# A two-layer recurrent transformer on one core: whole-unit loops become a hand-written order of pieces, with half-size weight loads

## The chip, the cores and the metric

The kernel runs on one core of a Trainium2 chip. The time is device microseconds from the first to the last instruction, as the median of several executions. Times inside the kernel are from a hardware profile of one execution. Engine names are those of the profile: PE is TensorE (matmuls), PEld its weight loads, DVE the vector engine, ACT the scalar engine, POOL is GpSimd, and SP the queue that issues the weight transfers.

## What is computed

There are two kinds of layer, A and B, applied as A, B, A, B, each with a layer norm before it and a residual after it. The sequence is 2048 tokens of 640 numbers. A is a memory-augmented attention that runs over the sequence in 64 segments of 32 tokens; the first 8 output rows of a segment are the memory that goes in front of the next segment, so the segments follow one another:

```python
for s in range(n_seg):                                   # 64 segments
    h = concat([mem, x[:, 32*s : 32*s+32]])              # 8 + 32 rows of 640
    q, k, v = h @ Wq, h @ Wk, h @ Wv                     # 32 heads of 192
    p = softmax(where(mask, q @ k.T * 192**-0.5, -1e9))
    o = (p @ v) @ Wo                                     # back to 640
    mem, out = o[:, :8], o[:, 8:]
```

B is a sliding attention with 32 heads of 20: each token looks at itself and the 7 tokens 2, 4, ... 14 places before it. Both A layers use the same weights, and so do both B layers. Inputs and weights are bf16. A's four weight matrices hold 31.5 MB[...], so part of them is read again for every segment.

## The kernel before

**Lanes and steps.** The two A layers are run at once, as two lanes of one step: lane 0 works on segment t of the first A layer, lane 1 on segment t-2 of the second. One step t does A for both lanes (80 columns: 2 x 40 rows) and B for the step before (64 columns). Steps 0 and 1 have only lane 0, steps 64 and 65 only lane 1, and step 66 has only B. The 62 steps between are full.

**Units.** A's 32 heads are handled as 8 groups of 4 heads (`NQUAD`). For each group i there are four weight units of 960 KB: K, Q, V and O. A projection (`proj_stationary`) is 30 matmuls with a fresh 128x128 weight block each, into one PSUM bank. Of the 32 units, every other one in order of use is resident on chip after the first step (`resident_units`, 16 units); the other 16 come in each step through a ring of four buffers (`RING`). The SP queue issues these loads in order of use, each one as soon as its buffer's last reader is done (`unit`).

**One group of heads.** K is copied out of PSUM by ACT into `KF` and `Kz` (L223 to L225), Q by DVE (`QT`, L230), V by ACT (`VT`, L236). V is transposed by six TensorE instructions (`a_vt`, L242) and copied by DVE (`Vt`, L246). Scores are eight matmuls (`a_s`, L256 and L257), then an exponential on ACT (`E`, L259) and a mask on DVE (`Em`, L261). `a_pv` sums the denominators by a matmul with ones (L270), multiplies `Em` by `Vt` (L275), takes the reciprocal of the denominators as two ACT operations (`R`, L278 and L279) and scales into `OT` with three DVE operations (L281 to L283). `a_o` is 30 matmuls that add into one accumulator bank, `acc` (L294).

**The end of a step.** When the last `a_o` is done, `mem_out` copies the memory rows of `acc` into the next step's input `hT` (L309), and `b_x1` adds the residual (L355). The next step's first K projection needs these memory rows. The layer norm for the next step's tokens (`ln1_sq`, `ln1`, `ln1_r`, `ln1_apply`) lies in the last group.

**Order.** The instruction order is the program's order, engine by engine (`manual_schedule`). `step` writes it as a loop over the groups: K, Q, V of group i, the output matmuls of group i-2, the transposes of V of group i, PV of group i-1, the scores of group i, with B's parts put in at fixed groups. Each function issues its matmuls and at once the ACT and DVE work that takes them out of PSUM. The output matmuls of the last three groups come together at the end:

```python
self.a_vt(7)
self.a_o(5, (0, 2, 3, 5))
...
self.a_pv(7)
self.a_o(5, (1, 4))
self.a_o(6)
self.a_o(7)
```

Most PSUM results rotate over four banks (`big`); scores, denominators, PV and `acc` have a bank each.

Of the kernel before, what the change touches and what calls it, by code (L numbers as in the profile page):

```python
# [17 lines left out]
P = 128  # L18
# [20 lines left out]
N_UNITS = 32  # L39
N_RES = 16  # L40
RING = 4

def unit_order():
    order = []
    for i in range(NQUAD):
        order.append(("k", i))
        order.append(("q", i))
        order.append(("v", i))
        if 2 <= i < NQUAD - 1:
            order.append(("o", i - 2))  # L50
    order += [("o", 5), ("o", 6), ("o", 7)]
    return order

def resident_units():
    res = set()
    for n, u in enumerate(unit_order()):
        if (n * N_RES) // N_UNITS != ((n + 1) * N_RES) // N_UNITS:
            res.add(u)
    return res

class Kernel:
    def __init__(self, ctx, tc, xT, m0T, wA, wqkv, wo, out):
        self.tc = tc
        self.nc = tc.nc
        self.x = xT
        self.mem0 = m0T
        self.wA = wA
        self.b_src = (wqkv, wo)
        self.out = out
        self.n_seg = 4 * xT.shape[0]  # L70
        pool = lambda name, bufs, **kw: ctx.enter_context(tc.tile_pool(name=name, bufs=bufs, **kw))
        self.cp = pool("consts", 1)
        self.wres = pool("wres", 1)
        self.wring = pool("wring", RING)
        self.ap2 = pool("act2", 2)
        self.ap3 = pool("act3", 3)
        self.bp = pool("bact", 1)
        self.xp = pool("xio", 1)
        self.ps_big = pool("ps_big", 4, space=PSUM)
        self.ps_one = pool("ps_one", 1, space=PSUM)  # L80
        self.units = {}
        self.held = (None, None)
        self.place = {u: n for n, u in enumerate(unit_order())}
        self.resident = resident_units()
        self.build_consts()

    def build_consts(self):
# [31 lines left out]
        self.On = pers("On", [P, 3 * P], 1)[0]  # L119
        self.YT = pers("YT", [P, NC, P], 1, zero=False)[0]  # L120
# [55 lines left out]
    def unit(self, kind, i):  # L176
        if (kind, i) in self.units:
            return self.units[(kind, i)]
        if self.held[0] == (kind, i):
            return self.held[1]  # L180
        res = (kind, i) in self.resident
        if res:
            t_ = self.wres.tile([P, 3840], BF16, name=f"w_{kind}{i}")
        else:
            t_ = self.wring.tile([P, 3840], BF16, name="w_ring")
        self.nc.sync.dma_start(out=t_[:], in_=self.wA[self.place[(kind, i)]])
        v = t_[:].rearrange("p (a b) -> p a b", a=6 if kind == "o" else NC)
        if res:
            self.units[(kind, i)] = v
        self.held = ((kind, i), v)  # L190
        return v

    def big(self, name):
        return self.ps_big.tile([P, 512], F32, name=name, tag="big")
# [9 lines left out]
    def proj_stationary(self, kind, i, t):  # L204
        nc = self.nc
        w = self.unit(kind, i)
        hT = self.hT[t % 2]
        ps = self.big(f"ps_{kind}")
        c0, c1 = self.cs.start, self.cs.stop
        for n in range(6):  # L210
            for c in range(NC):
                nc.tensor.matmul(ps[:, NT * n + c0:NT * n + c1], lhsT=w[:, c, P * n:P * (n + 1)], rhs=hT[:, NT * c + c0:NT * c + c1],  # L212
                                 start=(c == 0), stop=(c == NC - 1))
        return ps

    def a_k(self, i, t):
        nc = self.nc
        ps = self.proj_stationary("k", i, t)
        pv = ps[:, 0:6 * NT].rearrange("p (a b n) -> p a b n", a=2, b=3)
# [7 lines left out]
    def a_q(self, i, t):  # L227
        ps = self.proj_stationary("q", i, t)
        qt = self.ap2.tile([P, 6, NT], BF16, name="QT")
        self.nc.vector.tensor_copy(out=qt[:, :, self.cs], in_=ps[:, 0:6 * NT].rearrange("p (a n) -> p a n", a=6)[:, :, self.cs])  # L230
        self.qt = qt

    def a_v(self, i, t):
        ps = self.proj_stationary("v", i, t)
        vt = self.VT[i % 2][:, 0:6 * NT].rearrange("p (a n) -> p a n", a=6)
        self.nc.scalar.copy(out=vt[:, :, self.cs], in_=ps[:, 0:6 * NT].rearrange("p (a n) -> p a n", a=6)[:, :, self.cs])  # L236

    def a_vt(self, i):
        nc = self.nc
        ps = self.ps_big.tile([P, 6, P], BF16, name="ps_vt", tag="big")  # L240
        for n in range(6):
            nc.tensor.transpose(out=ps[:, n, :], in_=self.VT[i % 2][:, NT * n:NT * n + P], identity=self.ident[:])  # L242
        src = ps[0:NT].rearrange("p n e -> p (n e)").rearrange("p (a j e) -> p a j e", a=2, j=2)
# [4 lines left out]
    def a_s(self, i):  # L248
# [3 lines left out]
        kf, kz, qt = self.KF[i % 2], self.Kz[i % 2], self.qt  # L252
        cs, w = self.cs, self.cs.stop - self.cs.start
# [4 lines left out]
        e = self.ap2.tile([P, 4, NT], BF16, name="E")  # L258
        nc.scalar.activation(out=e[0:NT, :, cs], in_=sv[0:NT, :, cs], func=ACT.Exp, scale=float(DH) ** -0.5)  # L259
        em = self.ap2.tile([P, 4, NT], BF16, name="Em")  # L260
        nc.vector.tensor_tensor(out=em[0:NT, :, cs], in0=e[0:NT, :, cs], in1=self.maskA[0:NT, cs].unsqueeze(1).to_broadcast([NT, 4, w]), op=ALU.mult)  # L261
        self.em = em

    def a_pv(self, i):
        nc = self.nc
        em = self.em
        vt = self.Vt[i % 2]
        cs = self.cs
        dn = self.one("d")[:, 0:4 * NT].rearrange("p (h n) -> p h n", h=4)[:, :, cs]
        nc.tensor.matmul(dn, lhsT=self.ones[0:NT, :], rhs=em[0:NT, :, cs], start=True, stop=True)  # L270
        ops = self.one("o")
        ov = ops[:, 0:6 * NT].rearrange("p (a b n) -> p a b n", a=2, b=3)
        for pr in range(2):
            for (b, w0, j, st, sp) in [(0, 0, 0, True, True), (1, 128, 0, True, False), (1, 256, 1, False, True), (2, 384, 1, True, True)]:
                nc.tensor.matmul(ov[:, pr, b, cs], lhsT=vt[0:NT, 512 * pr + w0:512 * pr + w0 + P], rhs=em[0:NT, 2 * pr + j, cs], start=st, stop=sp)  # L275
        r = self.ap2.tile([P, 2, 2, NT], F32, name="R")
        rf = r[:].rearrange("p a b n -> p (a b) n")[:, :, cs]
        nc.scalar.activation(out=rf, in_=dn, func=ACT.Ln)  # L278
        nc.scalar.activation(out=rf, in_=rf, func=ACT.Exp, scale=-1.0)  # L279
        ot = self.ap3.tile([P, 2, 3, NT], BF16, name="OT")  # L280
        nc.vector.tensor_tensor(out=ot[:, :, 0:3:2, cs], in0=ov[:, :, 0:3:2, cs], in1=r[:, :, :, cs], op=ALU.mult)  # L281
        nc.vector.tensor_tensor(out=ot[0:64, :, 1, cs], in0=ov[0:64, :, 1, cs], in1=r[0:64, :, 0, cs], op=ALU.mult)
        nc.vector.tensor_tensor(out=ot[64:P, :, 1, cs], in0=ov[64:P, :, 1, cs], in1=r[64:P, :, 1, cs], op=ALU.mult)  # L283
        self.ots[i] = ot

    def a_o(self, i, ms=(0, 2, 3, 5, 1, 4)):
        nc = self.nc
        w = self.unit("o", i)
        ot = self.ots[i][:].rearrange("p a b n -> p (a b) n")
        if i == 0:  # L290
            self.acc = self.one("acc")
        for m in ms:
            for c in range(NC):
                nc.tensor.matmul(self.acc[:, NT * c + self.cs.start:NT * c + self.cs.stop], lhsT=w[:, m, P * c:P * (c + 1)], rhs=ot[:, m, self.cs],  # L294
                                 start=(i == 0 and m == ms[0] and c == 0), stop=(i == NQUAD - 1 and m == ms[-1]), skip_group_check=True)
# [4 lines left out]
    def mem_out(self, t):  # L300
        nc = self.nc
        a = self.lanes(self.acc[:, 0:NC * NT])
        h = self.lanes(self.hT[(t + 1) % 2][:, 0:NC * NT])
        if t + 1 == LAG:
            nc.vector.tensor_copy(out=h[:, :, 0, 0:NM], in_=a[:, :, 0, 0:NM])
            nc.vector.tensor_copy(out=h[:, :, 1, 0:NM], in_=self.m0T[:])
# [43 lines left out]
    def b_x1(self, b):  # L350
# [6 lines left out]
        self.bsq = self.ln_sq(x1)  # L357

    def b_ln(self, b):
        self.bmr = self.ln_r(self.ln_mv(self.ln_stats(self.x1[b % 2], self.bsq)))  # L360
# [15 lines left out]
    def b_k(self, b):  # L376
        ps = self.b_proj(b, D, "ps_bk")
        self.nc.scalar.copy(out=self.KB[:, :, 64 * (b % 2):64 * (b % 2) + NX], in_=ps[:, 0:NBC * NX].rearrange("p (a n) -> p a n", a=NBC))

    def b_q(self, b):  # L380
        ps = self.b_proj(b, 0, "ps_bq")
        qb = self.bp.tile([P, NBC, NX], BF16, name="QB")
        self.nc.scalar.copy(out=qb[:], in_=ps[:, 0:NBC * NX].rearrange("p (a n) -> p a n", a=NBC))
        self.qb = qb

    def b_v(self, b):
# [8 lines left out]
        nc.scalar.copy(out=self.VTB[:, :, hs], in_=ps[:, 0:NC * NX].rearrange("p (a n) -> p a n", a=NC))  # L395

    def b_vt(self, b):
        nc = self.nc
        ps = self.ps_big.tile([P, NC, P], BF16, name="ps_bvt", tag="big")
        for n in range(NC):  # L400
            nc.tensor.transpose(out=ps[:, n, :], in_=self.VTB[:, n, :], identity=self.ident[:])
        hs = slice(64 * (b % 2), 64 * (b % 2) + NX)
        src = ps[hs].rearrange("p n e -> p (n e)").rearrange("p (a h d) -> p a h d", a=2, d=BD)
# [3 lines left out]
    def b_qexp(self, g):  # L407
        nc = self.nc
        qx = self.ap2.tile([P, 2, BHC, NX], BF16, name="QX")
# [5 lines left out]
        if g == 0:  # L415
            self.eb = self.bp.tile([P, BH // 2, 2, NX], BF16, name="EB")

    def b_s(self, b, c):
# [4 lines left out]
        e = self.ap2.tile([P, BHC, NX], BF16, name="eraw")  # L423
        nc.scalar.activation(out=e[:, 0:nh, :].rearrange("p h n -> p (h n)"), in_=ps[:, 0:nh * NX], func=ACT.Exp, scale=float(BD) ** -0.5)
# [9 lines left out]
    def b_pv(self):  # L434
        nc = self.nc
        W = 2 * BD + 1
        on = self.On[:, 0:D // 2].rearrange("p (h d) -> p h d", d=BD)
# [212 lines left out]
```

The softmax here doesn't subtract the row's maximum and nothing guards it: scores larger than these inputs give would overflow.

## Time and profile before

| | before |
|---|---|
| time, median of 4 runs | 3675.62 us (3668.48 to 3692.0) |
| span of the profiled execution | 3672.8 us |
| PE busy, weight loads busy | 3290.7 us (90%), 3160.4 us (86%) |
| DVE, ACT busy | 2039.3 us (56%), 1713.3 us (47%) |
| moved by DMA | 1074.62 MB, mean 293 GB/s |
| loads through the ring | 1056 of 960 KB, 5.9 us to landing at the median |
| mean granted TensorE clock | 0.986 |

Matmuls are pipelined: one is shown with about 200 ns, but the next starts some 36 ns later, so the busy share of PE hides short gaps. The chain of work that ended last counts each piece of TensorE work once, from start to the next start, and names what was waited for in the gaps; "issue" in it is time in which the engine waited for nothing that the profile shows. A line of the list of waits gives the engine and line that stood idle, what ended the wait, the total, the number of times and the longest.

### The profile page before, as it was taken

To read this page: it belongs to the slowest core of one execution; us is meant where nothing else is said; L and a number is where in the kernel's file an instruction comes from. 1 tells how busy PE (TensorE), PEld (TensorE's weight loads), DVE (VectorE), ACT (ScalarE), POOL (GpSimd) and SP (SyncE) were. 2 spreads that over 40 slices of the span, in tenths; PEclk is the share of its full clock that TensorE was granted. 3 is DMA by queue.
4 is the path that set the end of the run, shared out by engine and by line. 5 is a ranking of instruction groups with operands and counts; after the bars stand their busy time and mean duration, and the time that the engine had idled before them with its cause. 6 is when DMAs were issued, how large, how long until landed. Compare 5 with 4: busy or idle time off the path is not lost.

```text
span 3672.8 us, 188119 instructions
## 1 busy us (share of the span) xinstructions
PE 3290.7 (90%) x86394; PEld 3160.4 (86%) x86394; DVE 2039.3 (56%) x6223; ACT 1713.3 (47%) x4621; POOL 40.7 (1%) x150
## 2 busy tenths in 40 slices
PE   4899899999999999999999999998999998999987
PEld 4788888888988888988988888888888988888886
DVE  2455555555555555555555555555555555555554
ACT  1344444444444444544544444444444544444443
POOL 1000000000000000000000000000000000000000
PEclk7899999999999999999999999999999999999998
DMA  9887888878888888888888888888878888878785
GB/s 391 299 290 286 285 298 294 294 286 302 294 290 294 290 289 293 300 291 298 301 288 301 290 293 287 294 292 285 294 285 292 298 286 289 298 287 289 287 290 213
DMA packets 160201, 1074.62 MB, mean 293 GB/s; under 512 B 17840, under 2 KB 21936, under 8 KB 159280
## 3 DMA queue, kind: packets, MB, share of 16 engines
q1 hardware_dynamic: 154656, 1057.33, 79.9%
q8 instruction: 676, 11.08, 1.2%
q10 hardware_dynamic: 4752, 5.26, 0.4%
q14 instruction: 117, 0.96, 0.1%
HBM read 1059.89 MB, written 2.62 MB: 289 GB/s over the span
## 4 chain that ended last, share of the span: by engine, by line
PE 83%; DVE 6%; issue 5%; ACT 4%; DMA 2%; POOL 0%; POOLq 0%; SPq 0%; ACTq 0%; DVEq 0%
PE ps_k L212 15%; PE ps_v L212 15%; PE ps_acc L294 14%; PE ps_q L212 14%; PE ps_vt L242 5%; PE ps_o L275 4%; ACT VT L236 2%; DVE On L449 2%; PE ps_s L257 2%; PE ps_s L256 2%; PE ps_d L270 2%; PE ps_by L467 2%; PE ps_bq L372 2%; PE ps_bk L372 2%; PE ps_bs L422 2%
## 5 line engine op out<-in xcount | busy, mean ns | idle before, releaser
L212 PEld LDWEIGHTS <-w_ring 128*128 128x128 bf16 x29700 | 1123.8, 100 | 122.4 <-issue 105.2
L246 DVE COPY Vt<-ps_vt 80x384 bf16<-80x384 bf16 x1056 | 325.2, 347 | 666.2 <-PE ps_vt L242 663.1
L212 PE MATMUL ps_k<-hT,w_ring 128*128 128x80 bf16 (+1 forms) x13860 | 573.6, 201 | 63.5 <-issue 28.2
L212 PE MATMUL ps_v<-hT,w_ring 128*128 128x80 bf16 (+1 forms) x13860 | 574.3, 201 | 42.7 <-issue 37.5
L294 PE MATMUL ps_acc<-OT,w_o 128*128 128x80 bf16 (+1 forms) x13860 | 586.2, 202 | 28.6 <-issue 23.1
L236 ACT CAST VT<-ps_v 128x480 bf16<-128x480 f32 (+1 forms) x528 | 288.3, 546 | 688.2 <-PE ps_v L212 688.2
L212 PE MATMUL ps_q<-hT,w_q 128*128 128x80 bf16 (+1 forms) x13860 | 572.8, 201 | 26.9 <-issue 21.8
L294 PEld LDWEIGHTS <-w_o 128*128 128x128 bf16 x13860 | 530.0, 100 | 34.7 <-issue 28.6
L212 PEld LDWEIGHTS <-w_q 128*128 128x128 bf16 x13860 | 521.7, 100 | 31.9 <-issue 26.0
L230 DVE CAST QT<-ps_q 128x480 bf16<-128x480 f32 (+1 forms) x528 | 338.9, 642 | 350.0 <-PE ps_q L212 344.1
L223 ACT CAST KF<-ps_k 128x320 bf16<-128x320 f32 (+1 forms) x528 | 220.3, 417 | 530.5 <-PE ps_k L212 525.0
L278 ACT ACTIVATE R<-ps_d 128x320 f32<-128x320 f32 (+1 forms) x528 | 226.9, 430 | 508.0 <-PE ps_d L270 507.9
L281 DVE TENSOR_TENSOR OT<-ps_o,R 128x320 bf16<-128x320 f32 (+1 forms) x528 | 253.5, 480 | 207.9 <-ACT R L279 175.1
L242 PE MATMUL ps_vt<-ident,VT 128*128 128x128 bf16 x3168 | 270.5, 222 | 71.1 <-ACT VT L236 65.1
L275 PEld LDWEIGHTS <-Vt 80*128 80x128 bf16 x4224 | 213.3, 99 | 112.7 <-DVE Vt L246 85.5
L242 PEld LDWEIGHTS <-VT 128*128 128x128 bf16 x3168 | 190.7, 99 | 88.6 <-ACT VT L236 81.5
L275 PE MATMUL ps_o<-Em,Vt 80*128 80x80 bf16 (+1 forms) x4224 | 245.3, 200 | 9.0 <-issue 2.8
L279 ACT ACTIVATE R<-R 128x320 f32<-128x320 f32 (+1 forms) x528 | 244.1, 462 | 16.6
L259 ACT ACTIVATE E<-ps_s 80x320 bf16<-80x320 f32 (+1 forms) x528 | 220.7, 418 | 9.3 <-PE ps_s L257 6.7
L257 PE MATMUL ps_s<-QT,Kz 128*128 128x80 bf16 (+1 forms) x2112 | 217.6, 200 | 2.6 <-issue 2.6
L256 PE MATMUL ps_s<-QT,KF 128*128 128x80 bf16 (+1 forms) x2112 | 217.9, 200 | 0.0
L270 PE MATMUL ps_d<-Em,ones 80*128 80x320 bf16 (+1 forms) x528 | 158.2, 300 | 55.4 <-DVE Em L261 53.7
(99 smaller groups left out, 3794.4 us busy)
## 6 DMA issues: line engine op xcount, KB each, us to landing
w_ring<-in_wA_dram SPq DMA_DIRECT2D x1056, 960.0 KB, 5.9
w_q<-in_wA_dram SPq DMA_DIRECT2D x7, 960.0 KB, 16.2
w_o<-in_wA_dram SPq DMA_DIRECT2D x7, 960.0 KB, 18.6
XT<-in_xT_dram ACTq DMA_DIRECT2D x16, 160.0 KB, 4.7
out_dram<-YT ACTq DMA_DIRECT2D x16, 160.0 KB, 3.4
wqkv_sb<-in_wqkv_dram SPq DMA_DIRECT2D x1, 2400.0 KB, 23.4
w_k<-in_wA_dram SPq DMA_DIRECT2D x1, 960.0 KB, 11.4
w_v<-in_wA_dram SPq DMA_DIRECT2D x1, 960.0 KB, 14.7
```

The source lines that it names most:

```text
L212: nc.tensor.matmul(ps[:, NT * n + c0:NT * n + c1], lhsT=w[:, c, P * n:P * (n + 1)], rhs=hT[:, NT * c + c0:NT * c + c1], start=(c == 0), st ...
L230: self.nc.vector.tensor_copy(out=qt[:, :, self.cs], in_=ps[:, 0:6 * NT].rearrange("p (a n) -> p a n", a=6)[:, :, self.cs])
L236: self.nc.scalar.copy(out=vt[:, :, self.cs], in_=ps[:, 0:6 * NT].rearrange("p (a n) -> p a n", a=6)[:, :, self.cs])
L242: nc.tensor.transpose(out=ps[:, n, :], in_=self.VT[i % 2][:, NT * n:NT * n + P], identity=self.ident[:])
L246: nc.vector.tensor_copy(out=dst[:, 512 * pr:512 * pr + 640].rearrange("p (j e) -> p j e", j=2)[:, :, 0:DH], in_=src[:, pr])
L256: nc.tensor.matmul(sv[:, h, cs], lhsT=kf[:, NT * h:NT * h + P], rhs=qt[:, 3 * pr + 2 * j, cs], start=True, stop=False)
L257: nc.tensor.matmul(sv[:, h, cs], lhsT=kz[:, NT * h:NT * h + P], rhs=qt[:, 3 * pr + 1, cs], start=False, stop=True)
L270: nc.tensor.matmul(dn, lhsT=self.ones[0:NT, :], rhs=em[0:NT, :, cs], start=True, stop=True)
L275: nc.tensor.matmul(ov[:, pr, b, cs], lhsT=vt[0:NT, 512 * pr + w0:512 * pr + w0 + P], rhs=em[0:NT, 2 * pr + j, cs], start=st, stop=sp)
L279: nc.scalar.activation(out=rf, in_=rf, func=ACT.Exp, scale=-1.0)
L281: nc.vector.tensor_tensor(out=ot[:, :, 0:3:2, cs], in0=ov[:, :, 0:3:2, cs], in1=r[:, :, :, cs], op=ALU.mult)
L294: nc.tensor.matmul(self.acc[:, NT * c + self.cs.start:NT * c + self.cs.stop], lhsT=w[:, m, P * c:P * (c + 1)], rhs=ot[:, m, self.cs], star ...
```

## The change

The loop in `step` is replaced by a list of about 180 names, `ORDER`, which is walked once per step. Each name is a piece: either some TensorE work (`K3`, `T3`, `S3`, `PO3`, `Oa3`, ...) or an operation on ACT or DVE that takes a result away (`KE3`, `VE3`, `TE3`, `EM3`, `R3`, `OT13`, ...). Every old function is cut into such pieces, so that the matmuls and the operation that reads their result can stand apart. This is for keeping TensorE supplied: other TensorE pieces lie between a result's producer and the piece that needs what was made of it. Groups are no longer taken strictly in turn (Q1 before Q0, V2 right after V0, V6 before V5).

```diff
+ORDER = """
+K0 K0y K0z K1 bst KE0 Q1 Q0 KE1 bmv QE1 br QE0 V0 bap V2 S0 VE0 E0 T0 bq VE2 bv bk EM0 S1 TE0 bqE bvE PD0 R0
+qx1 K2 Q2 KE2 V1 qx0 QE2 bkE E1 PO0 bs0 VE1 bs1 S2 EM1 K3 K4 OT10 be1 be0 bs2 PD1 KE3 OT20 KE4 E2 qx2 T1 TE1
+Q3 V3 eb0 PO1 QE3 be2 bt btE eb1 T2 R1 VE3 TE2 K5 S3 OT11 E3 bs3 Oa0 Q4 EM2 EM3 KE5 OT21 PD2 eb2 bs4 be3 R2 V4
+Q5 be4 PO2 QE4 PD3 VE4 eb3 bs5 eb4 QE5 S4 be5 OT12 T3 R3 TE3 Oa1 E4 V6 OT22 T4 eb5 S5 VE6 TE4 EM4 PO3 Ob0 bp1
+on1 V5 bp0 Oa2 OT13 PD4 OT23 on0 VE5 Q6 R4 E5 PO4 K6 Ob1 EM5 QE6 KE6 PD5 Q7 OT14 S6 bo T5 K7 boE OT24 E6 QE7
+R5 TE5 by PO5 EM6 byE Ob2 OT15 V7 KE7 S7 VE7 T6 LSQ PD6 OT25 Oa3 T7 E7 Ob3 TE6 PO6 EM7 R6 TE7 OT16 PD7 R7 OT26
+lst LMV Oa4 Ob4 PO7 OT17 Oa5 Ob5 OT27 Oa6 Ob6 O7x LR O7y LAP MEMa O7z MEMb X1 BSQ
+""".split()
```

Names in small letters, and those with L, are B's pieces and the layer norm of the next step; a digit is the group (in `OT1` and `OT2` the first digit is the part of OT).

Weights are handled in halves. A unit of 960 KB becomes two of 480 KB (three of the six column blocks of K, Q and V, or three of the six row blocks of O), each with its own load. 36 of the 64 halves are resident; the 28 that are streamed are chosen at equal steps of TensorE's time along the list, by `resident_halves`, which uses a table of piece lengths that stands in the program. The ring still has four buffers, now of a half each, so ring and resident halves together take 40 x 3,840 bytes per partition, and before 20 x 7,680, the same.

```diff
-N_UNITS = 32
-N_RES = 16
 RING = 4
+N_RES = 36
+O_ROWS = ((0, 2, 3), (5, 1, 4))
...
-            t_ = self.wring.tile([P, 3840], BF16, name="w_ring")
+            t_ = self.wring.tile([P, 1920], BF16, name="w_ring")
```

The end of a step is cut finer. The last output unit runs by column chunk instead of by row block, in three pieces, and the copy of the memory rows is cut in two, so that the next step's K0, which now also runs chunk by chunk over its first half, can start on the chunks whose memory is there.

```diff
+    def a_o7(self, part):
+        if part == "x":
+            self.w7 = [self.half("o", NQUAD - 1, h) for h in range(2)]
+        for c in {"x": (0, 1, 2), "y": (3,), "z": (4,)}[part]:
+            for h in range(2):
+                for k, m in enumerate(O_ROWS[h]):
+                    self.o_mm(self.w7[h], NQUAD - 1, k, m, c, last=(h == 1 and k == 2))
...
+    def k0(self, t):
+        self.kp[0] = self.big("ps_k")
+        self.w0 = self.half("k", 0, 0)
+        self.proj(self.kp[0], self.w0, 0, [(n, c) for c in range(NC - 1) for n in range(3)], t, True)
+
+    def k0y(self, t):
+        self.proj(self.kp[0], self.w0, 0, [(n, NC - 1) for n in range(3)], t, True)
...
+            elif n[:3] == "MEM":
+                if nt < T:
+                    self.mem_out(t, *((0, 3) if n == "MEMa" else (3, NC)))
```

Buffers are named by hand instead of taken in turn from a pool (`QT`, `E`, `Em`, `R`, `QX`, `eraw` two each, `OT` three), since their order of use is no longer the order of the groups. The rotation over four PSUM banks stays, in the order in which the pieces ask for them. The step's input (`x_take`) is copied at the start of the step instead of in group 5. The number and the shapes of the matmuls, of the ACT and DVE operations and of B's work stay, but for the memory copy, which is now two.

## The prediction

> **What bounds the kernel now.** I read the page from the top, then TensorE's waits over the full steps alone, then the chain through the end of one step, then that step in windows.
>
> The busy shares (part 1), the engine line of the chain (part 4) and three DMA queues (part 3):
>
> ```profile
> PE 3290.7 (90%) x86394; PEld 3160.4 (86%) x86394; DVE 2039.3 (56%) x6223; ACT 1713.3 (47%) x4621; POOL 40.7 (1%) x150
> ...
> q1 hardware_dynamic: 154656, 1057.33, 79.9%
> q8 instruction: 676, 11.08, 1.2%
> q10 hardware_dynamic: 4752, 5.26, 0.4%
> ...
> PE 83%; DVE 6%; issue 5%; ACT 4%; DMA 2%; POOL 0%; POOLq 0%; SPq 0%; ACTq 0%; DVEq 0%
> ```
>
> TensorE holds 83% of the chain. The other 17% is where it stands still, for the vector and scalar engines (10%), for "issue" (5%) and, at the start, for weights. The vector engine is at 56% and the scalar engine at 47%: neither is full, so a wait on them is a matter of order.
>
> Who kept TensorE waiting, from 140 to 3558 us (62 full steps: the memory copy that ends step 1 stands at 149.5 us, that of step 63 at 3552.1 us, so a step takes 54.9 us):
>
> ```profile
> PEld L212 <- issue: 117.2, 170, 2.4
> ...
> PEld L275 <- DVE Vt L246: 83.5, 63, 1.4
> PEld L242 <- ACT VT L236: 78.4, 125, 0.8
> ...
> PEld L456 <- DVE On L449: 39.1, 51, 0.8
> ...
> PE ps_k L212 <- DVE hT L309: 20.5, 62, 0.3
> ```
>
> Columns: microseconds in total, times, longest. Per step: 1.35 us for the transposed V, 1.26 for the copy VT, 0.63 for B's normalised output, 0.33 for the memory. "Issue" on all PEld lines of that answer sums to 161.6 us, 2.6 us a step. Total 6.2 us of the 54.9.
>
> The chain through the end of one step shows how such a wait arises:
>
> ```profile
> 2001.42 0.45 ACT R L278
> 2001.89 0.48 ACT R L279
> 2002.40 0.49 DVE OT L281
> 2002.89 0.22 DVE OT L282
> 2003.12 0.33 DVE OT L283
> 2003.48 0.32 DVE Em L261
> 2003.84 0.36 DVE Vt L246
> 2004.20 0.05 issue
> 2004.25 0.58 PE ps_o L275 x8
> ```
>
> Em and Vt stand behind OT in the vector queue, and OT waits for R. Their own inputs were there before: E ended at 2002.7 and the V transposes at 2002.3 us. They are late through queue order.
>
> **TensorE's own work per step**, from the lengths of the chain's pieces where nothing waits: 24 projections x 1.075 = 25.8; 240 output matmuls 8.6; V transposes 8 x 0.335 = 2.7; scores 8 x 0.29 = 2.3; denominators 8 x 0.14 = 1.1; PV 8 x 0.29 = 2.3; B's Q, K, V 0.88 + 0.88 + 0.73 = 2.5; B's scores 0.9; B's transpose, PV, output transpose and Wo 0.28 + 0.40 + 0.17 + 0.88 = 1.7; statistics 2 x 0.29 = 0.6. Sum 48.5 us. 48.5 + 6.2 = 54.7 against 54.9 measured, so the account closes.
>
> And the DMA side of the sample step:
>
> ```profile
> 1953.63:2007.67 54.04, 50.18 (x1310) 48.18 (x1309) 31.08 (x95) 26.43 (x70) 0.32 (x1) 1.00 0.83 298
> ```
>
> 298 GB/s at 83% busy: about 360 GB/s when busy. The clock is at 1.00, so no clock is to be gained or lost.
>
> **What the Trainium skill says.**
> - "Runtime: NRT & Kernel Launch", Instruction fetch mechanics: instructions are fetched in 16 KiB blocks of 256, by the sequencer's own DMA queue. The trace agrees: queue q8 moved 11.08 MB in 676 packets, 16.4 KB each, and the "issue" stalls lie at multiples of about 5.3 us, the time of 128 weight loads and 128 matmuls. So I read "issue" as a late block.
> - "DMA: Bandwidth & Descriptors", Queues, rings and completion order: an engine takes turns between queues by whole packets. That fits late blocks under weight traffic, but no number of this trace shows the turn itself.
> - "PSUM — Partial Sum Buffer", PSUM bank collisions: a bank is to be guarded as a whole, not by address. In the kernel before, nothing reads a bank that is still being written, so its trace is silent.
> - "TensorE: Matmul & The Clock Gate", Architectural detail: the scalar and vector queues are strict first-in-first-out. The chain above agrees (Em behind OT).
>
> **The change, part by part.**
>
> *Same arithmetic.* Matmuls, evictions, activations and vector operations per step stay, except that the memory copy is two (0.24 us once; I take two of 0.2) and the last output unit runs by column. TensorE's 48.5 us stay.
>
> *New order.* Each producer's eviction now has its own place, and its reader stands further away on TensorE. I summed the pieces along the list and set the eviction times of the rows beside the distances:
> - V0 ends at 5.7, T0 at 7.0: 1.4 us for a drain of about 0.2 and a 0.56 us VT copy. Before it was none. Gain 1.26.
> - TE7 is queued at 42.8, before OT1 6; the last PV is at 45.1. TE7 (0.69), OT1 6 (0.49) and OT2 6 (0.63) from about 43.1 end near 45.0: just in time. The other tight places (boE before by, KE5 before V4, LAP before the next K) keep 0.4 us or more. Gain 1.35.
> - On g0 is done near 33.5, its transpose at 36.8. Gain 0.63.
> - The four rotating PSUM banks: each is asked for four pieces later; along the list I find no reader that ends after its bank is wanted. Cost nothing, hidden by the projections between.
>
> I leave 0.1 for what such sums miss.
>
> *Step end.* K0 starts with the chunks that MEMa freed. With a guard by bank, MEMa waits for O7y, O7z for MEMa (drain 0.2, copy 0.2, two signals of 0.05: 0.5 us), and chunk 3 of K0 then waits about 0.15 for MEMb. Queued behind: all of TensorE. With a guard by address it would be about 0.2. I take 0.6; before it was 0.33 plus a refill of 0.17.
>
> *Half units, 36 of 64 resident.* 28 halves of 480 KB are streamed instead of 16 units of 960 KB: 13.8 MB a step instead of 15.7. At 51 us a step that is 270 GB/s, below today's 298. Rows are 3,840 B instead of 7,680; q10 with rows of 1,280 B costs 0.4% for 5.26 MB, q1 79.9% for 1057, the same per byte within its rounding.
>
> The ring still has four buffers, but of half the size. A half is wanted every 48.7/28 = 1.74 us, so a buffer comes round after 7.0 us; less 0.54 of use and 0.33 of issue (the median of the queue's DMA instructions) leaves 6.1 us. A whole unit landed in 5.9 us at the median, 4.5 at the least; half the bytes save 480 KB at 360 GB/s = 1.4 us, so 4.5 us. The tightest place in the list is from K2's first half to K3's second, 4.7 us apart: 3.8 are left, so up to 0.7 may show there. I take 0.3 a step, 0 to 4 at the ends.
>
> *Instruction fetch.* In the part of a step without waits (15 to 50 us after its start) the chain has 1.7 of the 1.8 us a step of its stalls over 0.15 us. With no waits anywhere this would spread over the whole step: 2.6 x 1.7/1.8 x 48.5/35 = 3.4 us if fetches stay as slow. But a weight transfer now puts 8 rows of 3,840 B on an engine at a time instead of 8 of 7,680, 1.3 us instead of 2.5 at 24 GB/s for one engine (391/16 at the start), and the stalls average 0.8 us. I take 1.3 us; both ends, 0.3 and 3.4, are kept.
>
> Full step: 48.5 + 0.1 + 0.6 + 0.3 + 1.3 = 50.8 us. 62 of them: 3150 us.
>
> *Start and tail.* Before: 149.5 + (3672.8 - 3552.1) = 270.2 us. Step 0 loads the same 34.9 MB and stays bound by them. Steps 1, 64 and 65 run one lane: about 36 us of TensorE work in 50.8 us, the rest waits and issue (1.2 to 2.5 us each in the chain there). I give each 7 to 8 us less, 22 in all: 248. The last B-only step keeps its serial chain.
>
> Sum 3150 + 248 = 3398, say **3400 us**.
>
> **Rivals.**
> 1. *The fetch takes the waits' place.* Late blocks stay as late: 48.5 + 0.1 + 0.6 + 0.3 + 3.4 = 52.9 us; with 262 for the ends 3542 us. For: the stalls sit where nothing else waits. Against: shorter turns, 9% less traffic per second.
> 2. *Everything is hidden.* Boundary 0.3, fetch 0.3, no DMA wait: 49.2 us, with 240 for the ends 3290 us. For: 2039 and 1713 us of work on the other engines. Against: single-lane steps show a stall at most blocks even after many small pauses.
> 3. *The ring is too shallow* (slower). If a half still takes 7 us to land, a buffer comes round in 7 + 0.9 us and 28 halves take 7 x 7.9 = 55 us; with 0.6 and fetch stalls 56 us, 3472 + 262 = 3734 us. For: half the bytes in flight. Against: 5.9 us was the median for twice the bytes.
>
> **Numbers.** Forecast (about 3345 to 3470) 0.50; rival 1 and what lies between 0.23; rival 2 0.19; rival 3 0.08, of which 0.05 is slower than before by over 0.5%, 0.02 within 0.5%. Range 3285 to 3565: it holds rivals 1 and 2 and leaves out rival 3 and the far tails. Faster 0.93, same 0.02, slower 0.05.
>
> **What would show it.** Right: the full step near 51 us; waits of TensorE for VT, Vt, Em and On gone from the list; at the step's end only MEMa and MEMb, about 0.6 us; "issue" below 2.6 us a step; halves landing in 4 to 5 us. Wrong: "issue" at 3 us or more (rival 1), TensorE waiting for w_ring (rival 3), or a new wait on a vector copy in the last 5 us of the step, where the sums are tight.

## The result, and the profile after

The changed kernel takes 3416.8 us (median of 11 runs, 3405.69 to 3436.86) against 3679.03 us for the kernel before (median of 16 runs): ratio 0.9289, 95% interval 0.9271 to 0.9308. The forecast was 3400 us.

The same lines of the page, now of the changed kernel (busy shares; three DMA queues with packets, MB and share of 16 engines; the chain by engine):

```profile
PE 3231.0 (95%) x86394; PEld 3144.1 (92%) x86394; DVE 2064.7 (60%) x6289; ACT 1727.1 (51%) x4621; POOL 40.8 (1%) x150
...
q1 hardware_dynamic: 271584, 929.59, 80.6%
q8 instruction: 676, 11.08, 1.3%
q10 hardware_dynamic: 4752, 5.26, 0.5%
...
PE 86%; DMA 10%; issue 3%; DVE 1%; POOL 0%; ACT 0%; SPq 0%; POOLq 0%; ACTq 0%
```

Work is the same: 86394 matmuls and 4621 ACT operations as before, 66 more on DVE (the second memory copy). The vector and scalar engines have all but left the chain (10% before, 1% now). The 10% of DMA is not idle time of TensorE: where a wait for a load ends the chain's piece, the chain runs back through the whole of that transfer. What TensorE really waited for is in its list of waits, here the weight-load side from 148.8 to 3300.6 us, the 62 full steps (total, times, longest):

```profile
PEld L250 <- issue: 56.4, 83, 1.9
PEld L364 <- issue: 32.6, 77, 1.1
PEld L250 <- DMA w_ring<-in_wA_dram: 22.7, 47, 1.3
```

The waits for Vt, VT and On, 199.7 us in the full steps before, are gone. A full step takes (3300.6 - 148.8)/62 = 50.8 us instead of 54.9.

The end of one step, from the chain of the changed kernel (start, length, what):

```profile
1976.98 2.06 PE ps_acc L364 x57
1979.03 0.02 issue
1979.06 0.22 DVE hT L396
1979.27 0.04 issue
1979.32 0.38 PE ps_acc L364 x6
1979.69 2.27 PE ps_k L250 x60
1981.96 0.29 PE ps_st L408 x10
```

The six matmuls after the copy are O7z. They add into another column chunk than the copy MEMa reads, and still wait for it: `acc` is guarded as a whole. After this stop they take 0.38 us, where six matmuls at 1.075 us for 30 take 0.215. 0.28 (the wait) + 0.17 + 0.12 (K takes 2.27 instead of 2.15) make 0.57 us for the boundary. The DMA side of this step:

```profile
1927.90:1979.30 51.40, 49.43 (x1309) 48.05 (x1309) 31.45 (x95) 26.48 (x70) 0.38 (x1) 1.00 0.82 270
```

270 GB/s instead of 298, at 82% busy, and the clock still at 1.00.

### The profile page after: what moved, and what is told of

It reads as the page before. It is cut to its first block, busy times and chain, and to the rows that moved or that the text cites. A ratio compares the mean times of both kernels' runs of the same rounds, so it can differ in the third digit from the quotient of the medians.

```text
span 3417.3 us, 189405 instructions
## 1 busy us (share of the span) xinstructions
PE 3231.0 (95%) x86394; PEld 3144.1 (92%) x86394; DVE 2064.7 (60%) x6289; ACT 1727.1 (51%) x4621; POOL 40.8 (1%) x150
## 4 chain that ended last, share of the span: by engine, by line
PE 86%; DMA 10%; issue 3%; DVE 1%; POOL 0%; ACT 0%; SPq 0%; POOLq 0%; ACTq 0%
PE ps_acc L364 16%; PE ps_q L250 15%; PE ps_v L250 15%; PE ps_k L250 15%; DMA w_ring<-in_wA_dram 9%; PE ps_vt L293 5%; PE ps_o L347 4%; PE ps_s L312 2%; PE ps_s L311 2%; PE ps_d L330 2%; PE ps_bk L456 2%; PE ps_by L571 2%; PE ps_bq L456 2%; PE ps_bv L475 1%; PE ps_bs L510 1%
## 5 line engine op out<-in xcount | busy, mean ns | idle before, releaser
L250 PE MATMUL ps_v<-hT,w_v 128*128 128x80 bf16 (+1 forms) x9900 | 442.0, 201 | 21.7 <-issue 17.8
L364 PE MATMUL ps_acc<-OT,w_ring 128*128 128x80 bf16 (+1 forms) x7920 | 398.9, 201 | 22.0 <-DVE hT L396 19.0
L250 PEld LDWEIGHTS <-w_v 128*128 128x128 bf16 x9900 | 385.2, 100 | 25.9 <-issue 21.5
L364 PE MATMUL ps_acc<-OT,w_o 128*128 128x80 bf16 (+1 forms) x7920 | 386.1, 201 | 11.6 <-issue 7.0
L250 PE MATMUL ps_k<-hT,w_k 128*128 128x80 bf16 (+1 forms) x8910 | 382.7, 201 | 6.8 <-issue 4.6
L250 PEld LDWEIGHTS <-w_k 128*128 128x128 bf16 x8910 | 341.2, 100 | 8.6 <-issue 5.6
L364 PEld LDWEIGHTS <-w_o 128*128 128x128 bf16 x7920 | 329.7, 99 | 17.1 <-issue 9.0
L250 PE MATMUL ps_k<-hT,w_ring 128*128 128x80 bf16 (+1 forms) x6930 | 321.0, 201 | 23.5 <-DMA w_ring<-in_wA_dram 11.4
L250 PE MATMUL ps_q<-hT,w_ring 128*128 128x80 bf16 (+1 forms) x6930 | 324.6, 201 | 18.3 <-DMA w_ring<-in_wA_dram 9.6
L250 PE MATMUL ps_v<-hT,w_ring 128*128 128x80 bf16 (+1 forms) x5940 | 276.3, 201 | 12.0 <-DMA w_ring<-in_wA_dram 7.8
```

Of the source, the lines that this page charges most:

```text
L250: nc.tensor.matmul(ps[:, NT * (n0 + n) + c0:NT * (n0 + n) + c1], lhsT=w[:, c, P * n:P * (n + 1)], rhs=hT[:, NT * c + c0:NT * c + c1], star ...
L364: self.nc.tensor.matmul(self.acc[:, NT * c + self.cs.start:NT * c + self.cs.stop], lhsT=w[:, k, P * c:P * (c + 1)], rhs=ot[:, m, self.cs], ...
```

## The experiments

Twelve more kernels ran. Ratios are to the kernel before, from runs on the same chip. The waits are those of the weight-load side between 150 and 3250 us, in microseconds a step; "engines" are waits for the vector or scalar engine. (For the kernel before this gives an issue of 2.5; the prediction's 2.6 is from 140 to 3558 us.) In the changed kernel and those made from it, "issue" includes 0.4 us at the step end, at O7z, which the run without weight loads shows not to be a late block.

That the rest of "issue" is late instruction blocks can be read from the packet times in the traces. Queue q8 moved 676 packets of 16.4 KB, and TensorE's 172,788 matmuls and weight loads alone make 675 blocks of 256 instructions. Of the 805 "issue" waits over 0.5 us in the kernel before, the changed one and the nine others that stream all loads in up to two transfers, all but two end 1.1 to 1.7 us after one of these packets has landed (median 1.4).

| run | ratio (95% interval) | full step, us | issue | w_ring | engines |
|---|---|---|---|---|---|
| before | 1 | 54.9 | 2.5 | 0 | 3.2 |
| changed | 0.9289 (0.9271 to 0.9308) | 50.8 | 1.6 | 0.4 | 0 |
| half loads, old loop | 0.9737 (0.9709 to 0.9766) | 53.7 | 1.1 | 0.3 | 3.4 |
| new order, whole loads | 0.9789 (0.9756 to 0.9822) | 53.8 | 4.7 | 0 | 0 |
| transposes by V | 0.9374 (0.9347 to 0.9401) | 51.6 | 0.9 | 0.2 | 1.6 |
| one end | 0.9273 (0.9244 to 0.9302) | 50.9 | 1.7 | 0.5 | 0 |
| no weight loads (streamed halves left out) | 0.8868 (0.8854 to 0.8883) | 49.05 | 0.4 | 0 | 0 |
| half of the loads (14 halves a step left out) | 0.8913 (0.8898 to 0.8928) | 49.05 | 0.5 | 0 | 0 |
| two loads a half | 0.9167 (0.9149 to 0.9184) | 50.1 | 0.7 | 0.6 | 0 |
| ring of six, 34 resident | 0.9449 (0.9431 to 0.9467) | 51.8 | 2.8 | 0 | 0 |
| ring of four, 34 resident | 0.9747 (0.9719 to 0.9776) | 53.5 | 1.2 | 3.3 | 0 |
| before, two loads a unit | 0.9888 (0.9866 to 0.991) | 54.6 | 2.3 | 0 | 3.2 |
| two loads a half, ring of six | 0.9133 (0.911 to 0.9157) | 50.0 | 1.1 | 0 | 0 |
| four loads a half | 1.1557 (1.1531 to 1.1583) | 63.2 | 0.4 | 11.6 | 0 |

### The two parts alone

Half loads in the old loop:

```diff
-        w = self.unit(kind, i)
...
         for n in range(6):
+            w = self.half(kind, i, n // 3)
             for c in range(NC):
...
+N_RES = 36
```

> The old loop with half-size loads: 36 of 64 halves resident, a ring of four halves, no piece moved. Theory (the order removes the waits, the half loads only shorten the instruction-fetch stalls and cut the traffic by an eighth): the waits of 3.6 us a step for VT, Vt, On and the memory stay, issue falls from 2.6 to about 1.5 us a step, so a full step takes about 53.8 us and the run about 3610 us (ratio 0.98). Rival 1 (the half loads bring nothing by themselves): 3675 us within 0.5%. Rival 2 (they carry most of the gain): below 3540 us. If the ring of halves is too shallow for the old order, waits for w_ring of over 0.5 us a step appear.

3598.46 us against 3698.25 us for the kernel before, 2.6% less. The waits on the engines are still there, and the step of 53.7 us is what the theory gave (53.8). In part by luck: issue fell further than to the 1.5 us expected, to 1.1, and waits for w_ring of 0.3 us came, which the theory did not have. From the list of waits of this run:

```profile
PEld L277 <- DVE Vt L248: 77.7, 58, 1.4
PEld L244 <- ACT VT L238: 73.1, 116, 0.8
PEld L214 <- issue: 48.0, 99, 1.6
PEld L459 <- DVE On L452: 41.3, 53, 0.8
```

The new order with whole loads:

```diff
-N_RES = 36
+N_RES = 16
...
+    def half(self, kind, i, h):
+        v = self.unit(kind, i)
+        return v[:, 3 * h:3 * h + 3, :] if kind == "o" else v[:, :, 3 * P * h:3 * P * (h + 1)]
```

> The new order with whole units of 960 KB: 16 of 32 resident, the streamed ones at equal steps of TensorE's time but none of O0 to O3, a ring of four. Theory: waits on the vector and scalar engines gone as in the changed kernel, but fetch stalls of 3 us a step or more in their place (rival 1 of the prediction): a full step of 52 to 53 us, 3490 to 3550 us in all. Rival (the order brings everything, the size of the loads nothing): 3417 us within 0.7%.

3616.86 us: the rival falls, and the stall is larger than the theory's (a step of 53.8 us, above its 52 to 53). No wait on the vector or scalar engine is left, but:

```profile
PEld L266 <- issue: 99.0, 115, 2.8
PEld L380 <- issue: 95.0, 124, 2.6
PEld L472 <- issue: 23.5, 18, 2.2
PEld L363 <- issue: 12.7, 14, 1.8
```

Issue went from 2.5 to 4.7 us a step (4.3 without the step end), so of the 3.2 us that the order freed, more than half came back as late instruction blocks. Each part alone gave 2.6% and 2.1%, both together 7.1%. The halves are what lets the order pay. They change three things at once: the size of a transfer, the bytes asked for ahead (four buffers of 480 KB instead of 960) and the traffic (13.8 MB a step instead of 15.7). The new order with whole units in two transfers each, which would take the first by itself, was not run.

### One wait put back

```diff
-... QE0 V0 bap V2 S0 VE0 E0 T0 bq VE2 bv bk EM0 S1 TE0 bqE ...
+... QE0 V0 VE0 T0 bap V2 S0 E0 bq VE2 bv TE0 bk EM0 S1 bqE ...
-... V1 qx0 QE2 bkE E1 PO0 bs0 VE1 bs1 S2 EM1 K3 ... qx2 T1 TE1
+... V1 bkE VE1 T1 qx0 QE2 E1 PO0 bs0 bs1 S2 EM1 TE1 K3 ... qx2
```

> The changed kernel with the V transposes of two groups (0 and 1) put straight behind their V projections, as the old loop had them; the copies between moved along. Theory: each costs what it cost before, a drain of 0.2, a VT copy of 0.56 and a restart of 0.16 us, less nothing: 1.6 us a step, about 3515 us (ratio to the kernel before 0.957). Rival (the stall only takes the place of a fetch stall that would come anyway): under 0.8 us a step, below 3465 us.

The old wait is back, in the chain of this run as in the old profile:

```profile
1960.51 1.09 PE ps_v L250 x30
1961.60 0.02 issue
1961.62 0.57 ACT VT L287
1962.19 0.04 issue
1962.23 0.51 PE ps_vt L293 x6
```

It stands at 1.6 us a step, as the theory had it, but the step grew by 0.7 us only (50.83 to 51.56): issue fell from 1.6 to 0.9 and the waits for w_ring from 0.4 to 0.2. The rival holds. A pause of TensorE lets a late block or a late load catch up, so waits of different kinds don't simply add.

### The step end

```diff
-lst LMV Oa4 Ob4 PO7 OT17 Oa5 Ob5 OT27 Oa6 Ob6 O7x LR O7y LAP MEMa O7z MEMb X1 BSQ
+lst LMV Oa4 Ob4 PO7 OT17 Oa5 Ob5 OT27 Oa6 Ob6 O7x LR O7y O7z LAP MEMa MEMb X1 BSQ
```

> The changed kernel with the memory copies after the whole last output unit: O7x, O7y, O7z, then MEMa and MEMb. Theory (the bank of acc is guarded as a whole, so the fine cut wins nothing): TensorE waits at K0 instead of at O7z, the same 0.5 us a step, 3417 us within 0.4%. Rival (the cut hides part of the copy): 0.2 to 0.5 us a step more, 3430 to 3450 us.

0.9273 (0.9244 to 0.9302) against 0.9289: no difference. In the chain the wait moved from O7z to K0:

```profile
1982.37 3.24 PE ps_acc L364 x90
1985.63 0.22 DVE hT L396
1985.85 0.04 issue
1985.89 2.31 PE ps_k L250 x60
```

From the first of these 90 matmuls to the end of K takes 3.24 + 0.02 + 0.22 + 0.04 + 2.31 = 5.83 us. In the changed kernel the same work, in the step before the one shown above, is 3.03 + 0.02 + 0.22 + 0.04 + 0.38 + 2.27 = 5.96. Cutting the copy finer wins nothing while both chunks are in the one bank of `acc`.

### How far the traffic is behind the rest

```diff
         res = u in self.resident
+        if u in self.seen and not res:
+            kk = "o" if kind == "o" else "kqv"
+            return next(v for k, v in self.units.items() if k[0] in kk)
+        self.seen.add(u)
```

> The changed kernel with no weight loads after step 0: from step 1 on, the 28 streamed halves are left out and a resident half is used in their place, so the numbers that come out are not the reference's; all matmuls, copies and waits between engines stay. Theory (issue and the waits for w_ring both come from the weight traffic, the rest is TensorE's own work): issue and DMA waits vanish, a full step takes 49.1 to 49.4 us, 3290 to 3320 us in all. Rival (issue is a matter of TensorE's instruction rate, not of the traffic): issue stays above 1 us a step, 3370 us or more.

3270.37 us, a step of 49.05 us: TensorE's own 48.5 and the boundary of 0.57, and nothing else. The step is the theory's; the whole is below its 3290 to 3320 us, because the ends take 227 us here instead of 265.5. All that is left on the weight-load side:

```profile
PEld L371 <- issue: 25.2, 63, 0.4
PEld L415 <- issue: 0.5, 1, 0.5
PEld L354 <- DVE OT L367: 0.4, 2, 0.2
```

63 times 0.4 us, once a step, on the line of the output matmuls: this is O7z behind the memory copy, which the list puts under "issue". The late blocks proper are gone with the loads, though TensorE uses its instructions as fast here as in any run. So they come from the loads, not from that rate.

The same with `self.cut` for the condition, which holds every second streamed half:

```diff
-        if u in self.seen and not res:
+        if u in self.seen and u in self.cut:
```

> As the one without weight loads, but every second streamed half is still loaded (14 a step, half the traffic); for the other 14 a resident half is used. Theory: issue goes with the traffic, 0.4 us a step or less, no wait for w_ring, 3310 to 3345 us. Rival (a single transfer in the way makes a block late, whatever the mean traffic): issue about half of the changed kernel's, 0.8 us a step, 3350 to 3370 us.

3286.94 us, issue 0.5 us a step with the 0.4 of the step end: the theory's side, and even less than it gave. Late blocks don't go in proportion to the loads: at 14 loads a step there are almost none, at 28 they cost 1.2 us.

### Size, depth and traffic

```diff
-        self.nc.sync.dma_start(out=t_[:], in_=self.wA[self.place[u]])
+        for j in range(2):
+            self.nc.sync.dma_start(out=t_[:, 960 * j:960 * (j + 1)], in_=self.wA[self.place[u]][:, 960 * j:960 * (j + 1)])
```

> The changed kernel with every half loaded by two transfers of half the row each (1,920 B): the same traffic, but each transfer puts half as much on an engine at a time. Theory of the prediction (a fetch waits for the transfer that has its turn, so a shorter turn helps): issue falls from 1.6 to 1.0 us a step or less, 3380 us or less. Rival (traffic decides, not the size of a turn): 3417 us within 0.4%. Rival 2 (the smaller rows cost bandwidth): slower, waits for w_ring up.

3382.09 us: 0.9167 against 0.9289, 1.3% less than the changed kernel, at the same traffic and the same ring. The theory holds, though 2 us above its 3380: issue without the step end fell from 1.2 to 0.3 us. Part of it came back as waits for w_ring, 0.4 to 0.6.

```diff
-RING = 4
-N_RES = 36
+RING = 6
+N_RES = 34
```

> The changed kernel with a ring of six halves and 34 resident (30 streamed, 7% more traffic). Theory (the ring of four costs 0.4 us a step in waits for w_ring): these vanish, issue rises by about 0.1 us, 3395 to 3410 us. Rival (traffic weighs more than depth): issue rises by 0.4 us or more, 3417 us or above.

3483.83 us, slower than the changed kernel by 1.7%. The waits for w_ring went, but issue rose by 1.2 us a step, three times the least that the rival named. Two things changed here, the depth of the ring and the number of halves that are streamed. The same 30 streamed halves with a ring of four:

> The changed kernel with a ring of four but only 34 halves resident, so 30 are streamed: the traffic of the ring of six (7% more) at the depth of the changed kernel. The ring of six took 3484 us, with issue of 2.4 us a step instead of 1.2. Theory 1 (depth: the more weight bytes are asked for ahead, the later an instruction block): issue stays at 1.2 to 1.5 us a step, waits for w_ring rise, 3430 to 3460 us. Theory 2 (traffic alone): issue 2.2 us a step or more, and with the waits for w_ring 3490 us or more.

3601.62 us. Theory 1 is right about issue (1.2 us with the step end) and far off on the rest: the waits for w_ring are 3.3 us a step instead of 0.4.

```profile
PEld L250 <- DMA w_ring<-in_wA_dram: 127.7, 160, 2.7
PEld L364 <- DMA w_ring<-in_wA_dram: 61.5, 59, 2.0
PEld L364 <- issue: 29.7, 70, 1.4
```

Two more halves a step mean that buffers have to come round 0.5 us sooner (48.7/30 instead of 48.7/28, times 4), and the loads land in 5.1 us instead of 4.8 at the median: it seems that the ring of four was just deep enough at 28. So at 30 streamed halves the deeper ring is the faster one (0.9449 against 0.9747).

The sum of issue can't tell depth from traffic for the late blocks, since the waits for loads give the blocks time. The starts of the packets on q8 can. Set packet n, counted from 0, beside the moment at which TensorE starts its instruction 256n + 190; a packet takes 0.96 to 1.02 us at the median in every run, but it starts at a different time after that moment:

| run | from that moment to the packet's start, us (median) |
|---|---|
| no weight loads | 0.2 |
| half of the loads | 0.5 |
| changed (ring of four, 28 streamed) | 2.1 |
| ring of four, 34 resident (30 streamed) | 1.9 |
| ring of six, 34 resident (30 streamed) | 2.6 |
| two loads a half | 1.7 |
| two loads a half, ring of six | 2.0 |
| before | 2.3 |
| before, two loads a unit | 2.2 |
| new order, whole loads | 3.0 |

So a late block is one whose transfer starts late, not one that takes long. At the same 30 halves, six buffers instead of four delay it by 0.7 us; two more halves at four buffers don't delay it. On depth that is for theory 1.

```diff
-        self.nc.sync.dma_start(out=t_[:], in_=self.wA[self.place[(kind, i)]])
+        for j in range(2):
+            self.nc.sync.dma_start(out=t_[:, 1920 * j:1920 * (j + 1)], in_=self.wA[self.place[(kind, i)]][:, 1920 * j:1920 * (j + 1)])
```

> The kernel before, each unit of 960 KB loaded by two transfers of half the row (3,840 B): order, traffic and bytes asked for ahead unchanged, only the size of one transfer is that of the changed kernel. The old loop with half loads had issue of 1.1 us a step instead of 2.6. Theory 1 (the size of one transfer sets the stall): issue falls to 1.0 to 1.5 us a step, 3590 to 3620 us at a time of before of 3680. Theory 2 (traffic or bytes asked ahead set it): issue stays at 2.2 us a step or more, 3650 us or more.

0.9888, with issue at 2.3 instead of 2.5 us: theory 2 on the size of the stall, though 1.1% was won. With the transfers of the changed kernel but a full ring of whole units asked for ahead and the old traffic, most of the stall stays.

The split loads with the ring of six:

> The split loads (two transfers of 1,920 B rows a half) together with a ring of six and 34 resident. Alone the first took 3382 us (issue 0.3, waits for w_ring 0.6 us a step), the second 3484 (issue 2.4, no waits for w_ring). Theory 1 (with short transfers depth does no harm): issue under 0.6 us a step, no waits for w_ring, 3345 to 3375 us, the fastest of all. Theory 2 (depth and traffic weigh on short transfers too): issue 1 us a step or more, 3395 us or more.

3376.14 us, 0.9133 (0.911 to 0.9157), the fastest of those that load every half, though its interval overlaps that of the split loads alone. Beside the ring of six with whole halves, only the size of a transfer differs, and neither waits for w_ring. The two longest "issue" lines of each, whole halves first:

```profile
PEld L250 <- issue: 72.4, 99, 3.1
PEld L364 <- issue: 47.3, 96, 1.7
...
PEld L365 <- issue: 32.3, 78, 1.2
PEld L251 <- issue: 15.0, 35, 1.2
```

Issue goes from 2.8 to 1.1 us a step, without the step end from 2.4 to 0.7. It is between the theories: short transfers help a lot, and depth still weighs on them (blocks start 2.0 us after their moment instead of 1.7; issue is 0.7 instead of 0.3, but there waits for w_ring give the blocks time). The mean rate of the transfers is not what decides: this run moves the most, 301 GB/s from 200 to 3200 us, against 289 with whole halves.

Four loads a half, by the same edit with four pieces of 480 columns:

> The changed kernel with every half loaded by four transfers of 960 B rows. Theory (shorter still): the rest of issue, 0.3 us a step, goes, but the share of busy time of the transfer engines rises (80.6% to 83.9% from one to two transfers), waits for w_ring rise from 0.6 to 1 us a step or more: 3380 us or above, no better than two transfers. Rival: 3365 us or less.

4275.49 us, slower than before by 16%. Issue is down to the step end, as the theory had it, and the waits for w_ring are up, but by another cause and far more:

```profile
PEld L251 <- DMA w_ring<-in_wA_dram: 448.3, 1023, 2.3
PEld L365 <- DMA w_ring<-in_wA_dram: 120.8, 327, 1.6
```

It is the queue that issues:

```profile
1999.96 64.75 SPq L228 DMA_DIRECT2D w_ring<-in_wA_dram  x115
```

115 issues in 64.75 us are 0.56 us each. This line merges issues and does not show the waits between them; the list of SP's own waits does. From 150 to 3250 us the queue waits for free buffers and earlier transfers 80% of the time in the changed kernel, 46% with two loads a half and 9% with four. So with 112 loads a step it is hardly ever free, and takes 63.2 us for them. The transfer engines are 80% busy here at 222 GB/s, less than the 90% of the run before; at that pace (278 GB/s when busy) they would need about 50 us for the 13.8 MB of a step, an estimate.

## Why the prediction was right

**TensorE's own work, 48.5 us a step.** Shown: with the loads left out the step is 49.05 us, 48.5 and the boundary.

**Order, 3.2 us of waits on the engines to 0.1.** Right: 0.2 us of such wait in 3,151.8 us. The tight place named, OT1 6 and OT2 6 before the last PV, shows there once: 0.2 us at one PV, and no more.

**Step end, 0.6 us.** Right at 0.57, and by a guard of the whole bank, as the Trainium skill advises ("PSUM — Partial Sum Buffer", PSUM bank collisions); the chain shows O7z waiting for a copy of other columns. `acc` is one buffer with a bank to itself, so no run here tells a guard by bank from a guard by buffer.

**Waits for w_ring, 0.3 us.** Measured 0.4. Landing was put at 4.5 us from half the bytes and 360 GB/s when busy, and measured at 4.8: from 200 to 3200 us the engines moved 276 GB/s at 83% busy, so 333 when busy. As the prediction had it, the shorter rows are not the reason: the kernel before with the same rows of 3,840 B moved 354 (294 at 83%). One thing that differs there is that twice as many bytes are asked for ahead. The place was not where the prediction looked: of the waits for w_ring in the full steps, on the matmul side of the list, 15 are at Q, 9 at V and 4 at K. That the rival of the shallow ring was close, the run with 30 streamed halves shows.

**Instruction fetch, 1.3 us.** Measured 1.2 without the step end. That late blocks would take the place of waits if the loads stayed whole is shown by the order alone (4.3 us, above the 3.4 of the rival), and that shorter transfers help by the pair with the ring of six. The Trainium skill's account of turns by whole packets ("DMA: Bandwidth & Descriptors", Queues, rings and completion order) agrees with that in direction, as do blocks that start late and then take no longer than without loads. But size alone does little in the old loop (2.5 to 2.3): the size of a turn, which the prediction gave as its reason, is not the whole mechanism. The bytes asked for ahead count too, which the prediction left out and the starts of the blocks show. So the 1.3, chosen between 0.3 and 3.4, was in part luck. What stays open is how much of the gain from whole units to halves is each of the two, and how much the smaller traffic.

**Start and tail, 248 us.** Too low: 148.8 + 116.7 = 265.5 us, where 270.2 stood before. The term was mis-sized by 17.5 us, nearly all of what separates the sum of 3398 from the profiled 3417.3 us. The two last A steps were given 7 to 8 us less each and got 2.4: 96.3 us for both (3300.6 to the last output matmuls at 3396.9), after 101.2. The waits on the engines went (3.9 to 0.2 us on the weight-load side in these two steps), but late blocks did not shrink with them: issue is 19.5 us, and was 20.0. A block of 128 pairs lasts 3.2 us there instead of 4.6 (0.75 us for 30 pairs instead of 1.075), and the chain shows stalls of 1.3 to 2.2 us again and again. Without weight loads the same two steps take 73.9 us, so it is the loads that hold these blocks up too. Step 1 was as long as before.

## What to carry to other kernels

When an engine's stream is made denser, look at what used its pauses to catch up: here instruction fetches, and more than half of what the order freed went back to them until the loads were halved, and with them the bytes asked for ahead. Taking a wait away is worth its length less what then moves into its place, and parts that look small alone can be worth more together (2.6% and 2.1% made 7.1%). The size of a transfer, the number asked for ahead and the time to issue one have to be set together: half loads split in two gave 1.3% more, split in four cost 24% against the changed kernel. And when one setting is traded for another, as buffers for resident halves here, change each by itself before giving one of them the credit.

## What the runs showed of the hardware

An instruction block is not slow under weight traffic, it starts late: its transfer takes 0.96 us with or without loads, but starts 0.2 us after the reference moment without loads and 2.1 us after it in the changed kernel, and TensorE goes on 1.4 us after it has landed.

More depth in the ring delays the blocks: at 30 streamed halves six buffers instead of four removed every wait for a load and made blocks start 0.7 us later. There the deeper ring was still the faster by 3%, since the waits for loads cost more. Against the changed kernel, with 28 streamed halves and four buffers, it lost 1.7%, because late blocks cost 1.2 us a step more. Two streamed halves more at four buffers took the waits for loads from 0.4 to 3.3 us a step, so the ring stood at an edge that the mean share of busy time (83%) doesn't show.
